# GEGLU feed-forward on one core: the last stage's reload of stored sums as one load, its joins reordered, and the last weight sums loaded ahead of raw weights

## The chip, the cores and the metric

The kernel runs on one core of a Trainium2 chip. The metric is the device time of one execution in microseconds (us). The core has five engines with a queue each: PE (TensorE, matrix products), DVE (VectorE), ACT (ScalarE), POOL (GpSimd) and SP (SyncE, which here only issues DMAs). ACT issues some DMAs too.

## The reference

```python
B, S, Dm, Df = 1, 2048, 1024, 3584        # all bfloat16
g = einsum("bsd,df->bsf", x, w_gate)
u = einsum("bsd,df->bsf", x, w_up)
h = gelu(g) * u                           # tanh form
return einsum("bsf,fd->bsd", h, w_down)
```

Three matrix products: two of 2048 x 1024 by 1024 x 3584, and one of 2048 x 3584 by 3584 x 1024.

## The kernel before

**Products by seven instead of eight.** The kernel works in two passes (`ip` 0 and 1) over 1024 tokens each, in two halves `c` of 512. In each pass the matrices are cut in two along each dimension, and the quadrants of a product come from seven products of sums and differences of blocks in place of eight products of blocks (Winograd's form). For the down product of a pass, `down` (L894), the blocks of `h` are `h(kh, j, c)`: `kh` is the half of Df, `j` one of 14 blocks of 128 rows, `c` the half of tokens. Sums of `h` and of `w_down` are made by DVE while PE multiplies; sums of `w_down` that both passes use are stored in DRAM by pass 0 (`td`) and loaded again in pass 1.

**The stage at issue** is `down` of pass 1, the last 100 us or so. It takes steps; `step()` carries out what `agenda` lists for a step, in the order in which it was entered with `at(last, step, what, ...)`. Steps 0 to 27 are the products of raw blocks, 28 to 30 the first products of sums, 31 to 50 the function `apart` (one of the seven products, done by seven smaller ones again). Steps 51 to 65 go on with the products of sums: at loop index `t` (3 to 17) PE multiplies pair `t` into the banks `e`, and pair `t - 4` into the banks `c`. Steps 66 to 79 are the third loop, `t` = 0 to 13: PE multiplies what `make73` made for `j = t` into `e`, and for 3 <= t < 9 also that of `j = t - 3` into `c`. After the loop come the products of j = 6 to 13 into the four banks of `c`, one bank after the other.

What is prepared for these, and at which step:

- `load12` (L627) loads a pair of stored weight sums `q<-td` on SP (L642); for the last three, j = 11, 12 and 13, at steps 49, 50 and 51 (`LAST12`). `make12` (L645) makes the two sums of `h` that are multiplied by them, on DVE.
- `fetch73` (L658) loads the raw block j of `w_down` on SP (L662), at the step `RAW73[j]`. `make73` (L666) makes from it and from `h` three operands with three DVE instructions and copies the raw block to 32 bit on ACT (`xT<-raw`, L677, or `tb<-raw`, L133), at the step `LAST73[j]`.
- Two quadrants that `apart` and its counterpart in pass 0 gave are stored as halves of words in DRAM tensors `pt`. `turn_back(quad, n)` (L740) loads and transposes them back, eight DMAs (L745) for each of two quadrants: those of quadrant 0, from `pt[0]` and `pt[1]`, are issued from ACT's queue, those of quadrant 1, from `pt[2]` and `pt[3]`, from SP's. `join(quad, i, gt)` (L749) puts halves together on ACT (L750).
- `put_0(i)` (L759) finishes four tiles of the output of pass 0: it joins quadrant 0, adds the sum that pass 0 stored in `ud` and that `fetch_u3` (L755) loads back, on DVE (`st<-gt,u`), and stores the tile. `join_1(i)` (L764) joins quadrant 1 into a tile that the last stores add to `e`.
- `store` (L846) adds two operands on DVE (L121) and issues the tile to the output on SP (L850). The last twelve: four of `e` with `p5`, four of `e` with the joined quadrant 1, and four of `c` with `u2`, each as soon as its bank is done.

**What sets the order.** In this stage the instructions of an engine stand in the order in which the code issues them; each engine takes its queue in order, and an issue on SP that waits holds back all issues behind it. Each DMA is given one of eight completion semaphores in turn, SP's and ACT's together, and is issued only when the DMA that had it before has landed. Tiles come from pools: `kpool` (36 slots) and `spool` (13) for tiles of 128x512, `wpool` (3) for 1 MB tiles. Which slot a tile gets is decided while the program is built, and the first to write a slot waits for the last reader of what was there. In `wpool` go, in this order, the `tid` tiles of `apart`, two 1 MB loads of stored sums (`w<-td`, L631), the transposed words of quadrant 0, those of quadrant 1, and the joined quadrant 1.

Of the kernel before, what the change touches and what calls it, by code (L numbers as in the profile page):

```python
# [10 lines left out]
def kernel(  # L11
# [23 lines left out]
    nc = tc.nc  # L35
    ENG = mybir.EngineType
    ORDER = {ENG.SP, ENG.DVE, ENG.Pool, ENG.PE}
    P = nc.NUM_PARTITIONS
    bf16 = mybir.dt.bfloat16
    f32 = mybir.dt.float32  # L40
# [4 lines left out]
    ADD, SUB, MUL = ALU.add, ALU.subtract, ALU.mult  # L45
# [10 lines left out]
    N = 512  # L56
    NS = N // P
# [17 lines left out]
    LAST12 = [14, 15, 16, 29, 30, None, None, 41, 41, None, None, 49, 50, 51]  # L75
    LAST12S = [16, 18, 20, 34, 37, 40, 43, 45, 47, 49, 51, 53, 55, 57]
    BIG12L = (5, 9)
    RAW73 = [40, 40, 40, 40, 48, 48, 49, 50, 52, 53, 55, 57, 60, 60]
    LAST73 = [52, 53, 55, 57, 59, 61, 63, 65, 66, 68, 70, 71, 72, 73]
    LATE3 = 6  # L80

# [4 lines left out]
    wpool = ctx.enter_context(tc.tile_pool(name="w", bufs=3))  # L86
# [23 lines left out]
    def slot(shape, dtype, name, sums=False):  # L110
        return (spool if sums else kpool).tile(shape, dtype, name=name, tag="s" if sums else "k")
# [8 lines left out]
    def dve(out, a, b, op):  # L120
        nc.vector.tensor_tensor(out=out, in0=a, in1=b, op=op)  # L121
# [29 lines left out]
    def load_w(u, queue=nc.sync):  # L151
        f0 = u * 2 * P
        w = wpool.tile([P, 2, NKB, 2 * P], bf16, name="w")
        for i, src in enumerate((w_gate, w_up)):
            queue.dma_start(
                out=w[:, i],
                in_=src[:, f0 : f0 + 2 * P].rearrange("(ko ki) f -> ki ko f", ki=P),
            )
        return w
# [417 lines left out]
    ud = dpool.tile([P, NS, N], f32, name="ud")  # L577
# [160 lines left out]
    turned = {}  # L738

    def turn_back(quad, n):  # L740
        if n == 0:
            turned["tp", quad] = wpool.tile([P, NS, 2, N], u16, name="w")
        half, i = n // NS, n % NS
        queue = nc.sync if quad else nc.scalar
        queue.dma_start_transpose(  # L745
            out=turned["tp", quad][:, i, half], in_=pt[2 * quad + half][:, i * P : (i + 1) * P]
        )

    def join(quad, i, gt):  # L749
        nc.scalar.copy(  # L750
            out=gt.bitcast(u16).rearrange("p (h d l) -> p h d l", h=2, l=2),
            in_=turned["tp", quad][:, i].rearrange("p h (l d) -> p h d l", l=2),
        )

    def fetch_u3(i):  # L755
        turned["u3", i] = slot([P, N], f32, "u3")
        nc.sync.dma_start(out=turned["u3", i], in_=ud[:, i])

    def put_0(i):  # L759
        gt = slot([P, N], f32, "gt")  # L760
        join(0, i, gt)
        store(0, 1, i, 0, lambda st: dve(st, gt, turned.pop(("u3", i)), ADD))

    def join_1(i):  # L764
        if i == 0:
# [40 lines left out]
    def at(last, step, what, *args):  # L806
        agenda.setdefault((last, int(step)), []).append((what, args))

    for last in (False, True):
# [6 lines left out]
        for j in range(NJ):  # L816
            if (LAST12 if last else AT12)[j] is not None:
                at(last, (LAST12 if last else AT12)[j], load12, j, last)
            at(last, (LAST12S if last else AT12S)[j], make12, j, last)
            at(last, RAW73[j] if last else AT73[j] - 3, fetch73, j)  # L820
            at(last, (LAST73 if last else AT73)[j], make73, j, last)
# [8 lines left out]
        at(1, 2 * i, make_si, i)  # L830
    for n in range(2 * NS):
        at(1, 52 + n // 2, turn_back, 0, n)
        at(1, 59 + n, turn_back, 1, n)
    for i in range(NS):
        at(1, 61 + i, fetch_u3, i)
        at(1, 75 + i, put_0, i)
        at(1, 71 + i, join_1, i)
    moves = [(c, ko) for ko in range(KH) for c in range(2)]
    moves += [(c, ko) for c in (1, 0) for ko in range(KH, NKB)]
    sa = {}  # L840
# [5 lines left out]
    def store(ip, c, i, dc, put):  # L846
        st = slot([P, N], bf16, "st")
        put(st)
        r0 = (2 * ip + c) * N + i * P
        nc.sync.dma_start(out=out2[r0 : r0 + P, dc * N : (dc + 1) * N], in_=st)  # L850
# [177 lines left out]
    w = load_w(1)  # L1028
# [295 lines left out]
```

## Time and profile before

| | |
|---|---|
| median of 3 runs | 538.98 us (538.81 to 541.65) |
| profiled execution, whole | 540.3 us |
| its span, first to last instruction | 538.5 us |
| PE busy | 528.5 us (98%) |
| DVE busy | 404.4 us (75%) |
| ACT busy | 302.0 us (56%) |
| mean granted clock of PE | 0.997 |

The profile is of one execution. An instruction's line number is that of the kernel before, or of a helper (L145 is every product, L121 every addition on DVE). A tile is named without its number: `q` are sums and loaded sums, `w` a 1 MB tile, `st` an output tile, `gt` a joined tile, `bank` a PSUM bank. "x16" is a run of instructions of the same kind merged in one row. Idle time in brackets is that of the engine before the instruction, with what ended it; a wait for several things is put down to the last.

### The profile page before, as it was taken

What the parts mean: (1) busy time and instruction counts of PE and PEld (TensorE: products, weight loads), DVE (VectorE), ACT (ScalarE), POOL (GpSimd) and SP (SyncE); (2) the same over time, 40 slices, a digit from 0 to 9 for tenths busy, and PEclk for the clock granted to TensorE, in tenths of its full rate; (3) what the DMA queues carried; (4) which work ended last, traced back from release to release, by engine and by line L of the source; (5) the groups of instructions that cost most, each with busy time, mean ns of one, the idle gap of its engine ahead of it and who ended that gap; (6) DMA issues with size and microseconds to landing.
All of it is one profiled execution on the core that took longest, in us unless ns stands there. A gap on an engine that the chain in (4) does not pass through costs nothing.

```text
span 538.5 us, 7762 instructions
## 1 busy us (share of the span) xinstructions
PE 528.5 (98%) x2375; PEld 374.9 (70%) x2375; DVE 404.4 (75%) x645; ACT 302.0 (56%) x544; POOL 268.4 (50%) x259
## 2 busy tenths in 40 slices
PE   9999999999999999999999999999999999999994
PEld 5568686868686764688877586766867764777783
DVE  2988768787777786749699887657677599788947
ACT  3557686968686841015576776665666621281652
POOL 1079977979797960000005989695897600000000
PEclk9999999999999999999999999999999999999998
DMA  9695218685777699999997899937354699599764
GB/s 246 150 256 170 79 64 288 197 293 196 234 235 245 224 380 368 356 317 244 248 294 215 288 314 356 253 109 206 97 168 118 225 356 328 163 319 297 189 127 156
DMA packets 141161, 126.09 MB, mean 234 GB/s; under 512 B 31680, under 2 KB 119232, under 8 KB 141120
## 3 DMA queue, kind: packets, MB, share of 16 engines
q1 hardware_dynamic: 136768, 124.55, 76.3%
q10 hardware_dynamic: 4352, 1.05, 1.0%
q8 instruction: 19, 0.31, 0.2%
q14 instruction: 22, 0.18, 0.1%
HBM read 86.38 MB, written 31.06 MB: 218 GB/s over the span
## 4 chain that ended last, share of the span: by engine, by line
PE 89%; DMA 4%; DVE 3%; ACT 2%; issue 1%; SPq 0%; ACTq 0%; DVEq 0%
PE bank L145 88%; DMA w<-pt 2%; DVE q L121 2%; DVE st L121 1%; DMA raw<-in_w_down_dram 1%; ACT gt L750 1%; DMA q<-td 1%; PE bank L1057 1%; PE bank L1002 1%; ACT s L875 0%; ACT xT L733 0%; SPq L662 0%; DVE xT L121 0%; ACTq L1319 0%; ACT u L138 0%
## 5 line engine op out<-in xcount | busy, mean ns | idle before, releaser
L124 POOL TENSOR_TENSOR s<-w 128x512 fp32r<-128x512 bf16 x102 | 117.8, 1176 | 47.5 <-DMA w<-in_w_gate_dram 32.4
L145 PE MATMUL bank<-t,s 128*128 128x512 f32 x528 | 126.3, 392 | 0.0
L145 PEld LDWEIGHTS bank<-t,s 128*128 128x128 f32 x528 | 99.1, 188 | 21.6 <-POOL s L124 0.3
L145 PE MATMUL bank<-xT,w 128*128 128x512 bf16 (+1 forms) x504 | 110.2, 376 | 0.0
L145 PEld LDWEIGHTS <-w 128*128 128x128 bf16 x504 | 47.9, 98 | 58.0 <-issue 4.2
L213 ACT ACTIVATE g<-sum 128x512 f32<-128x512 f32 x81 | 51.5, 636 | 61.0 <-DVE sum L121 60.2
L138 ACT COPY p<-bank 128x512 f32<-128x512 f32 x98 | 55.0, 589 | 46.5 <-PE bank L145 46.4
L121 DVE TENSOR_TENSOR hT<-g,bank 128x512 bf16<-128x512 f32 x72 | 49.0, 687 | 17.6 <-ACT g L213 11.9
L124 POOL TENSOR_TENSOR s<-w,s 128x512 fp32r<-128x512 bf16 x50 | 58.1, 1181 | 0.4
L145 PE MATMUL bank<-q 128*128 128x512 f32 x224 | 56.5, 392 | 1.5 <-DMA q<-td 1.4
L124 POOL TENSOR_TENSOR s<-s,w 128x512 fp32r<-128x512 f32 x50 | 57.5, 1172 | 0.2
L121 DVE TENSOR_TENSOR bank<-bank,p 128x512 f32<-128x512 f32 x74 | 51.3, 695 | 5.7 <-PE bank L145 5.1
L145 PE MATMUL bank<-t,sa 128*128 128x512 f32 x216 | 54.9, 397 | 0.0
L145 PE MATMUL bank<-tb,s 128*128 128x512 f32 x216 | 54.3, 393 | 0.0
L199 POOL COPY seen<-t 128x1 f32<-128x1 f32 x2 | 0.4, 184 | 107.5 <-DVE t L121 107.5
L145 PEld LDWEIGHTS bank<-q 128*128 128x128 f32 x224 | 41.9, 188 | 11.4 <-DVE q L121 1.8
L145 PEld LDWEIGHTS bank<-t,sa 128*128 128x128 f32 x216 | 40.6, 188 | 9.1
L145 PEld LDWEIGHTS bank<-tb,s 128*128 128x128 f32 x216 | 40.5, 188 | 9.0 <-POOL s L124 0.3
L121 DVE TENSOR_TENSOR sum<-bank,p 128x512 f32<-128x512 f32 x54 | 37.0, 686 | 12.0 <-PE bank L145 10.8
L138 ACT COPY u<-bank 128x512 f32<-128x512 f32 x62 | 35.4, 596 | 17.5 <-PE bank L145 13.7
L133 ACT CAST tb<-raw 128x512 fp32r<-128x512 bf16 x20 | 12.3, 624 | 37.3 <-DMA raw<-in_w_down_dram 29.0
L133 ACT CAST sa<-w 128x512 fp32r<-128x512 bf16 x54 | 30.7, 617 | 2.6 <-DMA out_dram<-st 2.6
(121 smaller groups left out, 734.3 us busy)
## 6 DMA issues: line engine op xcount, KB each, us to landing
raw<-in_w_down_dram SPq DMA_DIRECT2D x72, 256.0 KB, 5.9
w<-in_w_gate_dram SPq DMA_DIRECT2D x27, 512.0 KB, 4.8
w<-in_w_up_dram SPq DMA_DIRECT2D x27, 512.0 KB, 6.1
td<-m SPq DMA_DIRECT2D x11, 768.0 KB, 5.0
q<-td SPq DMA_DIRECT2D x28, 256.0 KB, 5.3
pd<-xT SPq DMA_DIRECT2D x10, 512.0 KB, 5.6
w<-td SPq DMA_DIRECT2D x5, 1024.0 KB, 8.6
p<-pd SPq DMA_DIRECT2D x20, 256.0 KB, 4.9
```

What stands on the lines that cost most here:

```text
L121: nc.vector.tensor_tensor(out=out, in0=a, in1=b, op=op)
L124: nc.gpsimd.tensor_tensor(out=out, in0=a, in1=b, op=op)
L133: nc.scalar.copy(out=t, in_=src)
L138: nc.scalar.copy(out=t, in_=ps)
L145: nc.tensor.matmul(ps, lhsT=lhs, rhs=rhs, start=start, stop=stop, skip_group_check=True)
L199: nc.gpsimd.tensor_copy(out=seen, in_=tile[:, :1].bitcast(f32))
L213: nc.scalar.activation(g, src, ACT.Gelu_apprx_tanh)
L750: nc.scalar.copy(out=gt.bitcast(u16).rearrange("p (h d l) -> p h d l", h=2, l=2), in_=turned["tp", quad][:, i].rearrange("p h (l d) -> p h ...
L1002: nc.tensor.transpose(tp[:, ko, :], xn[i][:, ko * P : (ko + 1) * P], ident)
L1057: nc.tensor.matmul(bank[3][:, :cols], lhsT=warm[:, :P], rhs=warm[:, :cols], start=True, stop=True)
```

## The change

The four loads of `ud` become one of 1 MB into a tile of `wpool`, at step 63. Quadrant 0's transposes alternate between its two halves, and its joins and stores (`put_0`) move from steps 75 to 78 to steps 69 to 72, in front of quadrant 1's joins, which move from steps 71 to 74 to steps 74 to 77. Quadrant 1's transposes move from steps 59 to 66 to steps 63 to 70. The raw blocks j = 4 to 11 are loaded up to three steps later and j = 12, 13 one earlier, so that j = 4 and 5 come at the step of the last `load12` and the others behind it.

```diff
-    RAW73 = [40, 40, 40, 40, 48, 48, 49, 50, 52, 53, 55, 57, 60, 60]
+    RAW73 = [40, 40, 40, 40, 51, 51, 52, 53, 54, 55, 56, 57, 59, 59]
...
     def turn_back(quad, n):
         if n == 0:
             turned["tp", quad] = wpool.tile([P, NS, 2, N], u16, name="w")
-        half, i = n // NS, n % NS
+        i, half = n // 2, n % 2
...
-    def fetch_u3(i):
-        turned["u3", i] = slot([P, N], f32, "u3")
-        nc.sync.dma_start(out=turned["u3", i], in_=ud[:, i])
+    def fetch_u3():
+        turned["u3"] = wpool.tile([P, NS, N], f32, name="w")
+        nc.sync.dma_start(out=turned["u3"], in_=ud)
 
     def put_0(i):
         gt = slot([P, N], f32, "gt")
         join(0, i, gt)
-        store(0, 1, i, 0, lambda st: dve(st, gt, turned.pop(("u3", i)), ADD))
+        store(0, 1, i, 0, lambda st: dve(st, gt, turned["u3"][:, i], ADD))
...
     for n in range(2 * NS):
         at(1, 52 + n // 2, turn_back, 0, n)
-        at(1, 59 + n, turn_back, 1, n)
+        at(1, 63 + n, turn_back, 1, n)
     for i in range(NS):
-        at(1, 61 + i, fetch_u3, i)
-        at(1, 75 + i, put_0, i)
-        at(1, 71 + i, join_1, i)
+        at(1, 69 + i, put_0, i)
+        at(1, 74 + i, join_1, i)
+    at(1, 63, fetch_u3)
```

## The prediction

> **What bounds the kernel now.** I read the page first, then the chain of waits from its end backwards, then the timeline of the last 60 us, and last what the built programs of both kernels say each instruction waits for.
>
> ```profile
> span 538.5 us, 7762 instructions
> ...
> PE 528.5 (98%) x2375; PEld 374.9 (70%) x2375; DVE 404.4 (75%) x645; ACT 302.0 (56%) x544; POOL 268.4 (50%) x259
> ```
>
> PE is the bound: 538.5 - 528.5 leaves 10 us in which it does nothing. The chain of waits (start, length, what) says where those lie:
>
> ```profile
> 488.98 6.61 DMA w<-pt
> ...
> 495.66 3.58 DMA q<-td
> 499.23 0.14 issue
> 499.37 9.33 PE bank L145 x40
> ...
> 523.58 4.31 ACT gt L750 x4
> ...
> 531.60 4.18 DVE st L121 x7
> ```
>
> Two places. At 499.37 PE resumes after a load of stored weight sums (q<-td), whose issue had waited for a transposing DMA (w<-pt). From 523.58 on the chain leaves PE: joins on ACT, then stores on DVE. The timeline shows both, with the idle time before an instruction in brackets:
>
> ```profile
> 489.64 0.68 DVE L121 TENSOR_TENSOR q<-raw 128x512 fp32r<-128x512 bf16 x1
> 490.53 3.79 PE L145 MATMUL bank<-w,q 128*128 128x512 f32 x16
> 491.56 0.69 DVE L121 TENSOR_TENSOR q<-q,hT 128x512 fp32r<-128x512 f32 x1
> 494.70 0.69 DVE L121 TENSOR_TENSOR q<-q,hT 128x512 fp32r<-128x512 f32 x1
> 495.97 1.07 PE L145 MATMUL bank<-q 128*128 128x512 f32 x4
> 499.37 1.16 PE L145 MATMUL bank<-q 128*128 128x512 f32 x4 [1.43 <-DMA q<-td]
> 524.69 0.69 DVE L121 TENSOR_TENSOR st<-gt,u 128x512 bf16<-128x512 f32 x1 [8.05 <-ACT gt L750]
> 529.26 1.53 PE L145 MATMUL bank<-tb,q 128*128 128x512 f32 x6
> 535.10 0.68 DVE L121 TENSOR_TENSOR st<-bank,u 128x512 bf16<-128x512 f32 x1
> ```
>
> PE's last product ends at 529.26 + 1.53 = 530.79. The last store on DVE starts only at 535.10, because sixteen stores of 0.60 us each stand in a row from 524.69, and four of them (st<-gt,u, those of put_0) waited 8.05 us for ACT. What follows the last store start is fixed: 538.5 - 535.1 = 3.4 us.
>
> **1. The tail: put_0 ahead of the last sums.** In the changed program the four put_0 stand one by one between the triples that make73 makes for j = 9 to 13, so they leave the queue in front of the last twelve stores. They still cost 4 x 0.60 = 2.4 us of DVE. Their cover is the time in which DVE waits now (8.05 us); without it they would delay the sums that PE multiplies last. With twelve stores left, the first starts when the e sums are done (523.45 now) and eight of them take 4.9 us, to about 528.4; the four c stores then follow PE's quarters, and the last starts 0.05 us after PE's end. So the tail gives back 535.10 - 530.84 = 4.26 us as long as PE ends when it does now. What is late next is PE itself.
>
> **2. One load in place of four.** SP now issues four u<-ud (0.52, 0.53, 1.58 and 0.52 us) between transposes; they go, and one issue of 1 MB comes. It stands behind all raw loads and one transpose of pt2, and its issue waits for an earlier DMA on its completion semaphore (there are eight, handed out in turn) and for the product t = 10. I work out raw loads at 0.5 us an issue from 497.5, the transpose at 502.7 and this load at 503.9. Landing: the 1 MB loads w<-td took 6.9 and 8.6 us, the 256 KB loads u<-ud 3.6 to 4.7; 503.9 plus 5 to 8.6 is 509 to 512.5, and I take 510 because most raw loads have landed by then. The first put_0 is due on DVE at 510.9 (step 4). DVE is in order: behind it stand the sums for j = 10 to 13. The last of them is then made by 520.0, and PE wants it at 522.39 + 0.93 = 523.3, so the load may land 3.3 us late, at 514.2, for nothing.
>
> **3. The second quadrant.** Its transposes (1.12 us each on SP) run from about 502.7 to 513.2 instead of 504.4 to 519.6; its joins come last on ACT, four of 1.1 us, behind the cast that now waits for PE's c product of step t = 6 (516.1), so 516.7 to 521.2. DVE wants the first at about 526.3. Hidden, with 5 us in hand.
>
> **4. The loads of stored sums, and a reused buffer.** Here I look for what PE waits for at 499.37. The first two pairs of td loads (j = 11, 12) do move ahead of the raw loads, but the pair for j = 13, the one that PE waited for, still stands behind two raw loads and the pt2 writes. Its first issue now waits for the sixth of the eight transposes on ACT's queue. These transposes start earlier: the first shared a semaphore with a raw load that landed at 488.83 and now follows a load long landed, so it starts after ACT's cast at 484.64 + 0.62 = 485.3, not at 488.98. At 1.28 us each plus a cast in between the sixth starts at 492.5. If it lands in 2.9 to 5.3 us (SP's lone transposes took 2.7, ACT's later ones 4.3 to 5.3), the pair is issued at 495.4 to 497.8, 0.5 us apart, and the half that PE needs first lands 3.1 to 3.6 us after its own issue: 499.0 to 501.9. I take 499.2, since the raw traffic that slowed the present ones has moved behind. That alone is no gain on 499.23.
>
> The second part is a wait that the diff does not show. The pool gives the weight difference that make73 makes for j = 2 (the DVE instruction at 489.64) another buffer: that of the sum for j = 6, which PE reads until the end of the sixteen products of 490.53, at 494.32. Before, its buffer was long free. So this instruction starts at 494.36, 4.7 us later, and all that is queued behind it on DVE shifts. Two of those PE waits for. The sum for j = 12 starts 491.56 - 489.64 = 1.92 us after it and takes 0.69: 496.97, plus 0.2 for the weight load, 497.2 against PE's 495.97: 1.2 us of stall. The next eight products (1.82 us) end at 499.0. The sum for j = 13 starts 494.70 - 489.64 = 5.06 us after it: 500.11, plus 0.2, 500.3: 1.3 us more. PE thus resumes at 500.3 instead of 499.37: 0.93 us later than now, the present stall of 1.43 us being replaced by two of 2.5 us together. The cost is bounded by -1.43 (neither wait binds) and by the late end of the load, 501.9 + 0.1 - 499.37 = 2.6.
>
> After that DVE has no idle time until 520.7 (eighteen instructions of 0.604 us from 500.02 bring it to 510.9), and every raw load is due 2 us or more before its use. PE ends at 530.79 + 0.93 = 531.7.
>
> **5. Sum.** -4.26 (tail) + 0.93 (PE) = -3.3 us: a span of 535.2. The profiled execution took 540.3, its span and 1.8 us around it; 537.0 after. It was 1.3 us above the median of 538.98; the same saving from the median gives 535.6, or -0.6%. A change of 0.5%, 2.7 us, is about what a measurement of this kernel can tell from none: that line lies at 536.3, or a PE delay of 1.55 us in place of 0.93.
>
> **Rivals.**
>
> *Late weight sums* (PE delay of 1.55 to 7 us, no change to tell). If ACT's sixth transpose takes the 6.61 us of the first one now, it lands at 499.1; the pair's second half goes out at 499.6 and lands at 503.2 (3.6) to 504.8 (5.25, its twin's time): delay 3.9 to 5.5, time 538.6 to 540.2. For it: one DMA's landing frees the next issue all through this stretch. Against: 6.61 was with seven loads queued ahead, and those are gone. Such a wait is one gap of PE of about 4 to 5 us, and the clock could go with it. The row: PE stops at 530.79, and the granted clock holds until inside the second of these slices (the last three columns are clock, DMA share, GB/s):
>
> ```profile
> 534.00:535.00 1.00, 0.00 (x0) 0.00 (x0) 1.00 (x2) 0.00 (x0) 0.00 (x0) 1.00 0.57 194
> 535.00:536.00 1.00, 0.00 (x0) 0.00 (x0) 0.78 (x2) 0.00 (x0) 0.00 (x0) 0.82 0.65 217
> ```
>
> 0.82 is 0.36 us at half, so it fell at 535.64, 4.85 us after the last product; a gap below that costs nothing more by this row. [...]
>
> *No new wait binds* (delay under 0.5 us). The pool's buffer is free in time or PE is not as tightly fed as I read: PE resumes with the load at 499.3, time 534.6; with the load early too, PE ends at 529.4 and the time is 533.2. Against it stands a wait that is in the built program.
>
> *The single load blocks DVE* (slower). Four loads gave each put_0 its own landing; now all four hang on one, in front of sums that PE needs. Past 514.2 each us late is a us of the end. Slower by 0.5% (541.7) needs a landing after 520.3. With the pair landing at 504.8, the raw halves behind it, the load issued at 509 and 8.6 us of flight, it lands at 517.6 and the time is 539.0; it takes one more link of 3 us in SP's chain.
>
> *The change does not do what it says.* Partly so for the sums of j = 13, and that is in the forecast.
>
> **Numbers.** Forecast (delay 0.5 to 1.55, 534.9 to 536.3): 0.52. No new wait: 0.14. Late sums: 0.26. Blocked DVE, slower: 0.08. Faster by over 0.5% is the first two, 0.66; the same 0.26; slower 0.08. The range goes from the middle of the early case, 533.9, to the lower half of the late one, 538.4; it leaves out about 0.05 below and 0.15 above.
>
> **What would show it.** In the profile after: four st<-gt,w on DVE between 510 and 520 and no wait for ACT ahead of 524; the last DVE store within 0.1 us of PE's last product; an idle DVE of some 4 us ahead of the q<-raw after 489.6, released by PE; two gaps of PE between 496 and 500.5, released by DVE and not by q<-td; the 1 MB load landing before 512. One PE gap released by q<-td after 501 makes the late rival right; a DVE wait for the w<-ud load makes the blocked one right; no DVE wait at 490 to 494 makes step 4 wrong.

## The result, and the profile after

The changed kernel is slower: 543.12 us median (542.01 to 544.36, 10 runs) against 540.81 (538.37 to 541.66, 10 runs) for the kernel before, measured beside it. The ratio is 1.0053, 95% interval 1.0033 to 1.0072. The forecast was 535.6 us, range 533.9 to 538.4. It was counted from a median of 538.98 (3 runs), so what compares is its -0.6% with the +0.5% measured. The profiled execution took 542.01 us.

First the page of the changed kernel: its span, and what its engines were busy for.

```profile
span 540.2 us, 7756 instructions
...
PE 530.9 (98%) x2375; PEld 376.4 (70%) x2375; DVE 404.5 (75%) x645; ACT 302.1 (56%) x544; POOL 268.3 (50%) x259
```

PE executes the same 2375 products as before and is busy 2.4 us longer: some of them ran at a lower clock. The chain of waits (start, length, what) says where the end was decided:

```profile
493.24 2.90 DMA w<-pt
...
496.87 6.19 DMA q<-td
503.06 0.14 issue
503.19 33.69 PE bank L145 x136
536.88 0.02 issue
536.91 0.69 DVE st L121
```

After 503.19 there is nothing but PE, and one store behind it: the tail that the change went for is gone. In front of it stands the same link as before, a load of stored sums behind a transpose, and it now releases PE 3.8 us later. The timeline shows the rest:

```profile
490.32 3.79 PE L145 MATMUL bank<-w,q 128*128 128x512 f32 x16
494.15 0.69 DVE L121 TENSOR_TENSOR q<-raw 128x512 fp32r<-128x512 bf16 x1 [4.63 <-PE bank L145]
495.09 1.01 SPq L662 DMA_DIRECT2D raw<-in_w_down_dram  x2
496.20 1.05 SPq L642 DMA_DIRECT2D q<-td  x2
496.82 1.21 PE L145 MATMUL bank<-q 128*128 128x512 f32 x4 [0.90 <-DVE q L121]
499.28 0.69 DVE L121 TENSOR_TENSOR q<-q,hT 128x512 fp32r<-128x512 f32 x1
503.19 2.05 PE L145 MATMUL bank<-q 128*128 128x512 f32 x4 [4.23 <-DMA q<-td]
514.68 0.69 DVE L121 TENSOR_TENSOR st<-gt,w 128x512 bf16<-128x512 f32 x1 [1.34 <-ACT gt L750]
535.34 1.52 PE L145 MATMUL bank<-tb,q 128*128 128x512 f32 x6
536.91 0.69 DVE L121 TENSOR_TENSOR st<-bank,u 128x512 bf16<-128x512 f32 x1 [1.14 <-PE bank L145]
```

The DVE wait of 4.63 us for PE is the reused buffer of step 4, and it costs PE a first stall of 0.90 us. The second stall, due near 499 for a sum on DVE, is hidden under a larger one: PE stands for 4.23 us until the load lands. The four products at 503.19 then take 2.05 us where such a row took 1.16 before. The stretches (PE, PEld, DVE, ACT, POOL busy; then granted clock, DMA share, GB/s) say why:

```profile
502.00:504.00 2.00, 0.81 (x2) 0.74 (x3) 1.58 (x3) 0.00 (x1) 0.00 (x0) 0.50 1.05 324
504.00:506.00 2.00, 2.00 (x6) 1.52 (x6) 0.72 (x2) 2.00 (x5) 0.00 (x0) 0.50 1.02 327
506.00:508.00 2.00, 2.00 (x6) 1.55 (x5) 1.78 (x3) 1.08 (x3) 0.00 (x0) 0.51 1.06 350
508.00:510.00 2.00, 2.00 (x10) 1.65 (x9) 1.56 (x3) 0.00 (x0) 0.00 (x0) 1.00 0.77 170
```

The granted clock is one half until 508, and PE does 6 products in 2 us in place of 10.

**The sum.** Traces start some tenths apart, so I count from a common event, the start of the sixteen products `bank<-w,q`, to the last DVE store. Before: 535.10 - 490.53 = 44.57 us. Forecast: 3.33 less, 41.24. After: 536.91 - 490.32 = 46.59. PE was to resume 500.3 - 490.53 = 9.77 us into this stretch and resumed at 503.19 - 490.32 = 12.87, which is 3.10 late; from there the last store was to start 41.24 - 9.77 = 31.47 us later and started 33.72 later, which is 2.25 of lost clock. 3.10 + 2.25 = 5.35, the whole difference between 41.24 and 46.59.

### The profile page after: what moved, and what is told of

It reads as the page before. It is cut to its first block, busy times and chain, and to the rows that moved or that the text cites. A ratio compares the mean times of both kernels' runs of the same rounds, so it can differ in the third digit from the quotient of the medians.

```text
span 540.2 us, 7756 instructions
## 1 busy us (share of the span) xinstructions
PE 530.9 (98%) x2375; PEld 376.4 (70%) x2375; DVE 404.5 (75%) x645; ACT 302.1 (56%) x544; POOL 268.3 (50%) x259
## 4 chain that ended last, share of the span: by engine, by line
PE 93%; DMA 2%; DVE 2%; ACTq 1%; ACT 1%; issue 0%; SPq 0%; DVEq 0%
PE bank L145 92%; ACTq L745 1%; DMA q<-td 1%; DVE q L121 1%; PE bank L1057 1%; DMA w<-pt 1%; DVE xT L121 1%; PE bank L1002 1%; ACT s L875 0%; ACT xT L733 0%; ACT u L138 0%; DVE st L121 0%; ACT xT L677 0%; SPq L642 0%; ACTq L733 0%
```

## The experiments

Each ran in a group with the kernel before, and its ratio is against that. "Stretch" is the time just defined.

**`e1_tail_only`: the change without the new order of raw loads.**

```diff
-    RAW73 = [40, 40, 40, 40, 51, 51, 52, 53, 54, 55, 56, 57, 59, 59]
+    RAW73 = [40, 40, 40, 40, 48, 48, 49, 50, 52, 53, 55, 57, 60, 60]
```

> The change without its new load order (RAW73 as before); joins, transposes and the single 1 MB load as changed. Theory A (the loss is the load order: the last pair of sums lands late and PE's clock falls; the tail is a real gain): PE stalls at about 499.4 as in the kernel before, ends at 530.8, the last store follows at once, span about 534.3, 4 us (0.8%) under the kernel before. Theory B (the single load and the put_0 in front of the sums block DVE and so PE): DVE waits for the load ahead of the first put_0, PE loses products behind t = 9, span at or above 538.5.

535.54 us, ratio 0.9928 [0.9915, 0.9941], span 534.6, stretch 39.76: 4.81 us less than before. Of these, 3.70 lie between PE's resuming at 499.22 and the last store, where step 1 had 4.26; the other 1.11 are PE resuming that much earlier in the stretch. The tail's edits alone are a real gain.

```profile
499.22 1.16 PE L145 MATMUL bank<-q 128*128 128x512 f32 x4 [0.31 <-DMA q<-td]
513.47 0.69 DVE L121 TENSOR_TENSOR st<-gt,w 128x512 bf16<-128x512 f32 x1 [4.22 <-DMA w<-ud]
522.65 1.20 PE L145 MATMUL bank<-q 128*128 128x512 f32 x4 [0.22 <-DVE q L121]
```

The pair of sums is hardly waited for. DVE waits 4.22 us for the 1 MB load, and the idle time of PE behind that is 0.22 us.

**`e2_raw_only`: the new order of raw loads in the kernel before,** that is the first line of the change's diff and no other.

> The kernel before with the new load order alone (RAW73). Theory A: the last pair lands at about 503 as in the changed kernel, the clock falls to half for some 6 us, PE ends near 536.9; the stores then wait for PE and not for the joins, so the span is about that of the changed kernel, 540.2 (0.3 to 0.5% over the kernel before), although nothing of the tail is moved. Theory B: as the kernel before, 538.5, since what it blames is not in this kernel.

542.17 us, ratio 1.0056 [1.0034, 1.0078], stretch 45.62.

```profile
495.15 0.69 DVE L121 TENSOR_TENSOR q<-raw 128x512 fp32r<-128x512 bf16 x1 [4.63 <-PE bank L145]
497.83 1.21 PE L145 MATMUL bank<-q 128*128 128x512 f32 x4 [0.90 <-DVE q L121]
503.86 1.15 PE L145 MATMUL bank<-q 128*128 128x512 f32 x4 [3.89 <-DMA q<-td]
```

The wait for the buffer, the stall and the late pair are all there without any edit of the tail, and `e1_tail_only` has no DVE wait for PE near 494. So they come with the new order of raw loads: this one line of load steps turns the -0.7% of the tail alone into +0.5%.

**`e3_warm32` and `e7_warm44`: PE kept busy in the gap.** The changed kernel with products by zeros ahead of the step of j = 13, 32 and then 44 of them:

```diff
+            if last and t == NJ - 1:
+                for _ in range(32):
+                    matmul(e[0][:, : 2 * P], zero[:, :P], zero, False, False)
```

> The changed kernel with 32 products of zeros by zeros (128x256, bf16) added into bank e[0] just ahead of the products that wait for the last pair; they add nothing to the sums and fill some 3.5 of the 4.2 us of the gap. Theory A with the clock (half clock after the gap costs 2.3 us by itself): granted clock stays at 1.00 after 501, PE ends at about 534.6, span about 538.0, 2.2 us under the changed kernel. Without the clock (the late pair alone explains the loss, or the clock falls for another reason): clock still falls near 501.6, span 540.2 or a little more.

541.13 us, ratio 1.0041 [1.0023, 1.0059]. The profile didn't settle it. In that execution, the slowest of the eleven, the pair landed later still, PE idled 3.10 us behind the zeros, and the clock fell all the same, to 0.50 from 507.13 to 510.54. But 8 of its 11 runs have a mean clock of 0.999 or 1.000 and took 540.0 to 542.2 us, and the other three have 0.996 and took 543.6 to 544.2.

> The changed kernel with 44 products by a tile of zeros ahead of the step of j = 13, added to a sum that they do not alter (44 x 0.115 = 5.1 us of PE), so that PE is busy in the gap before the late pair whether it lands at 503 or at 505. Theory A (the clock fell because PE stood idle for over 2.6 us): PE starts the zeros near 499.2, ends them near 504.3, goes on within 1.5 us, the granted clock stays 1.00 from 500 to 530, and from the first product of j = 13 to PE's last end it takes 31.4 to 31.6 us instead of 33.7; span 538.8 to 539.5, ratio 1.000 to 1.003. Theory B (the clock falls for another reason here, such as the DMA traffic or the fp32 products): it falls to one half after 501 with the zeros in place, 33.7 us from resume to end, and the ratio is 1.005 to 1.009, as the zeros then delay PE by 1 us more.

541.23 us, ratio 1.0024 [1.0009, 1.0038]; the mean clock is 1.000 in all 10 runs.

```profile
500.00:502.00 2.00, 2.00 (x19) 1.76 (x19) 1.90 (x4) 0.62 (x1) 0.00 (x0) 1.00 1.24 278
502.00:504.00 2.00, 2.00 (x21) 1.79 (x19) 2.00 (x4) 0.62 (x1) 0.00 (x0) 1.00 0.89 271
504.00:506.00 2.00, 2.00 (x14) 1.54 (x12) 1.46 (x3) 0.47 (x1) 0.00 (x0) 1.00 0.98 286
506.00:508.00 2.00, 2.00 (x10) 1.64 (x9) 1.39 (x3) 2.00 (x6) 0.00 (x0) 1.00 0.97 304
```

PE is busy throughout and the clock stays. The products of j = 13 start at 505.02 and the last store at 536.51, 31.49 us later in place of the changed kernel's 33.72, though the same DMAs run beside it. So the idle gap took the clock, at 2.23 us. The late pair is still there: the span, 539.8, is 0.3 us above what theory A expected. The fill is no cure: it holds PE until 505, and the stretch, 44.92, is still longer than before.

**`e5_pair_first`: all pairs of last sums ahead of the pt2 writes and the raw loads,** in the changed kernel:

```diff
-    LAST12 = [14, 15, 16, 29, 30, None, None, 41, 41, None, None, 49, 50, 51]
+    LAST12 = [14, 15, 16, 29, 30, None, None, 41, 41, None, None, 49, 49, 49]
```

> The changed kernel with one list edited so that all three pairs of last stored sums, j = 11 to 13, go out at step 49, ahead of the pt2 writes and of the raw loads; the reused buffer, and with it the wait of the weight difference for j = 2, stays. Theory A (the loss is the late landing of the pair for j = 13 and the clock that fell in that gap; the buffer wait alone costs what step 4 of the prediction said): the pair now follows an early transpose on ACT's queue, which landed by 491.8 in the changed kernel, and lands before 498; DVE still waits 4 to 5 us for PE near 494; PE stalls near 496 and 499 for DVE alone, 2 to 2.5 us together, no gap is long enough for the clock, and PE's last products end 5 us earlier than in the changed kernel (2.9 for the landing, 2.25 for the clock): span 534.8 to 535.8, ratio 0.994 to 0.996. Theory B (the buffer wait costs more than its two stalls, since all of DVE shifts): PE stalls for DVE again after 505, ratio 0.998 or more. Theory C (moving loads here only moves the lateness to the pt2 writes and the transposes): ACT's casts wait behind the transposes, a sum for j = 13 is late for a cast as in e4_tail_p47, ratio near 1.001.

537.64 us, ratio 0.9959 [0.9942, 0.9975], span 536.0, stretch 41.87, and no loss of clock: the mean is 1.000.

```profile
494.67 0.69 DVE L121 TENSOR_TENSOR q<-hT,q 128x512 fp32r<-128x512 bf16 x1 [4.05 <-PE bank L145]
496.74 1.21 PE L145 MATMUL bank<-q 128*128 128x512 f32 x4 [0.30 <-DVE q L121]
499.94 1.19 PE L145 MATMUL bank<-q 128*128 128x512 f32 x4 [1.07 <-DVE q L121]
514.97 0.69 DVE L121 TENSOR_TENSOR st<-gt,w 128x512 bf16<-128x512 f32 x1 [1.55 <-DMA w<-ud]
524.14 1.19 PE L145 MATMUL bank<-q 128*128 128x512 f32 x4 [0.60 <-DVE q L121]
```

This is the picture that the prediction drew of the changed kernel: both gaps of PE are released by DVE. PE resumes 499.94 - 490.84 = 9.10 us into the stretch, against 8.84 before and 9.77 in the forecast: that is 0.26 us late in place of 0.93. Another DVE instruction stands at the head of the wait here, so that 0.60 us less of it reaches PE in the first stall (0.30 for 0.90). The pair landed at 498.84, later than the expected 498 but ahead of DVE's sum. The load for put_0 landed at 514.85, past the 514.2 up to which the prediction called it free, and there PE lost 0.60 us. The span came 0.2 us above what was expected.

**`e9_pair_before_raws`: only the raw loads of j = 4 and 5 taken from in front of the pair,** which stays behind the pt2 writes:

```diff
-    RAW73 = [40, 40, 40, 40, 51, 51, 52, 53, 54, 55, 56, 57, 59, 59]
+    RAW73 = [40, 40, 40, 40, 52, 52, 52, 53, 54, 55, 56, 57, 59, 59]
```

> The changed kernel with the raw loads of j = 4 and 5 taken from step 51 to step 52, so that the pair of sums for j = 13 stays behind the pt2 writes and beside the transposes, but no raw load stands in front of it; the reused buffer stays. Open is what made the pair's second load fly 6.19 us where the forecast had 3.1 to 3.6. Theory A (the two raw loads issued 1.1 and 0.5 us ahead of it): it now flies 3.3 to 4.2 us, lands by 500.5, PE resumes for DVE's sum near 500 or within 0.6 us of it, the clock holds, the ratio is 0.995 to 0.998, as e5_pair_first. Theory B (the DMA transposes on ACT's queue, two of which fly beside it as before): 5.5 to 6.5 us, it lands at 501.3 to 502.5, PE idles for 2.3 to 3.5 us, the clock falls where that is over 2.6 us, ratio 0.998 to 1.005.

541.35 us, ratio 1.0012 [0.9991, 1.0032]: not to be told from before. The load that PE needs flew 5.38 us (chain of waits):

```profile
496.50 5.38 DMA q<-td
501.88 0.14 issue
502.01 34.21 PE bank L145 x136
```

So the flight is long without the two raw loads too, and theory A falls. Theory B's landing, gap and ratio hold (the flight is just under its 5.5), but the transposes by themselves aren't the reason: in `e5_pair_first` and `e10_pair_first_four` the same load flew 3.40 and 3.36 us beside transposes of its own, issued 0.07 and 0.17 us ahead of it. What it has ahead in `e9_pair_before_raws` and not there is a pt2 write issued 1.4 us earlier and the pair's first half 0.9 us earlier. These don't settle it either, since the flight differs as much between executions with the same order of issues (pt2 write, two raw loads, pair). The chains of `e2_raw_only` and of `e3_warm32` have:

```profile
499.27 4.46 DMA q<-td
498.43 7.45 DMA q<-td
```

With the 6.19 us of the changed kernel that is 4.5 to 7.5 us for one order. In `e7_warm44` the pair was issued as late as 501.0 and flew 3.2 to 3.4. What makes the flight long stays open. What does go with the place in the queue is the landing, counted from the start of the stretch: 12.4 to 15.1 us in the four kernels with two raw loads ahead of the pair, 10.8 in `e9_pair_before_raws`, 8.0 and 10.0 with the pair first, 8.7 before.

**`e4_tail_p47`: `e1_tail_only` with the last three entries of `LAST12` at 47.**

> As the tail alone (RAW73 as before), and all three last pairs of stored sums are loaded at step 47, ahead of the raw blocks and of the transposes on ACT's queue (LAST12 ends 47, 47, 47). Theory A: the last pair lands by 492.5, no wait for it at all, so the present stall of 1.43 us goes too: PE ends at about 529.4, span about 533, 1% under the kernel before. If a raw block or a reused buffer becomes the next wait: 533.5 to 535.5. Theory B: no gain on the kernel before.

540.23 us, ratio 1.0015 [1.0002, 1.0028]: worse than `e1_tail_only`. The pair is no longer waited for, but what it passed is:

```profile
493.43 0.62 ACT L677 CAST xT<-raw 128x512 fp32r<-128x512 bf16 x1 [8.41 <-DMA pt<-xT]
499.36 0.69 DVE L121 TENSOR_TENSOR q<-hT,hL 128x512 fp32r<-128x512 bf16 x1 [3.38 <-ACT xT L677]
500.89 1.20 PE L145 MATMUL bank<-q 128*128 128x512 f32 x4 [3.21 <-DVE q L121]
```

ACT's casts stand in its queue behind transposes that were issued late; DVE waits for a cast, PE for DVE, and the clock is 0.50 from 502.05 to 505.46. The early load wasn't free here: ACT's queue hung on those it overtook.

**`e8_tail_p49`: the same pairs at step 49 instead.**

> e1_tail_only (the tail's edits alone, raw loads as before the change) with all three pairs of last stored sums at step 49, ahead of the pt2 writes. Theory A: in e1_tail_only PE waited 0.31 us for q<-td and 0.71 for a sum on DVE near 499; the first goes, the second stays unless ACT's cast comes earlier: 0.3 us gain or none, ratio 0.991 to 0.993, not to be told from e1_tail_only. Theory C (as in e4_tail_p47, earlier pairs push the pt2 writes, the transposes and ACT's casts later): a sum on DVE waits for an ACT cast by 2 us or more, PE stalls over 2.6 us and its clock falls, ratio 0.998 to 1.002.

534.49 us, ratio 0.9903 [0.9886, 0.9921], a little under the expected 0.991 to 0.993. In the chain of waits PE runs in one piece from 485.02:

```profile
485.02 46.23 PE bank L145 x201
531.28 0.69 DVE st L121
```

The stretch is 38.62 us: no wait of PE is left in it. Two steps divide this from `e4_tail_p47`.

**`e6_four_loads`, `e10_pair_first_four` and `e11_tail_p49_four`: the single load taken apart** in `e1_tail_only`, `e5_pair_first` and `e8_tail_p49`:

```diff
-        nc.sync.dma_start(out=turned["u3"], in_=ud)
+        for i in range(NS):
+            nc.sync.dma_start(out=turned["u3"][:, i], in_=ud[:, i])
```

> e1_tail_only with the 1 MB load of the first quadrant's stored sums taken apart again into four loads of 256 KB, one behind the other at the same step and into the same tile. Theory A (the place of the put_0 brings the gain, not the size of the load; the load has slack): ratio 0.991 to 0.995, as e1_tail_only; the four issues push the second quadrant's transposes back by 1.5 to 3 us, hidden, since the first of its joins has some 5 us; the first put_0 waits less than the 4.2 us that it waited for w<-ud there. Theory B (the single load is part of the gain, by three issues fewer on SP's queue and on its completion semaphores): the last join_1 or the last c stores wait for the transposes, the last store comes 1 to 3 us behind PE's end, ratio 0.995 to 0.999.

535.03 us, ratio 0.9913 [0.9898, 0.9929], stretch 38.61; DVE no longer waits for w<-ud.

> e5_pair_first with the 1 MB load taken apart into four of 256 KB. There the load flew 6.92 us and landed at 514.85, later than the 514.2 up to which the prediction called it free, the first put_0 waited 1.55 us for it, and PE lost 0.60 us to a sum near 524. Theory A (a late single load holds up DVE and through it PE): the first quarter lands by 512.5, no wait for w<-ud stands on DVE or one under 0.5 us, the 0.60 us near 524 go, and PE takes 32.0 to 32.2 us from the first product of j = 13 to its end in place of 32.71: ratio 0.994 to 0.996. Theory B (the 0.60 us come from the buffer wait's shift of DVE by itself): PE still waits 0.4 us or more for DVE near 524, ratio 0.995 to 0.997.

537.90 us, ratio 0.9958 [0.9942, 0.9973]. The first quarter landed at 511.80, no `st<-gt,w` waits for w<-ud, and the 0.60 us near 524 are gone, as theory A has it; the ratio doesn't tell this from `e5_pair_first`. The 32.0 to 32.2 us expected of PE weren't met: 33.07, since in this execution the pair landed at 500.33, PE idled 2.16 us and the clock fell; the clock at half for 3.41 us costs 1.7 of these, which leaves 31.4. That is 1.3 us under the 32.71 of `e5_pair_first`, of which the 0.60 are less than half; the rest isn't explained.

> The two edits that did no harm together: the tail's edits alone, raw loads as before the change, all pairs of last sums at step 49, four loads of 256 KB. Both e6_four_loads and e8_tail_p49 had PE without a gap from 485 to its end (46.23 us in each), so there is nothing left for either to take away there. Theory A: ratio 0.989 to 0.993, not to be told from those two; PE runs 46.2 us in one piece. Theory B (the two interact, transposes of the second quadrant come too late): the last join ends after 524, the last store comes 1 us or more behind PE's end, ratio 0.993 to 0.997.

535.38 us, ratio 0.9913 [0.9896, 0.9931], stretch 38.61. Four loads do as well as one in every pairing. `e1_tail_only`, `e6_four_loads`, `e8_tail_p49` and `e11_tail_p49_four` are 0.7 to 1.0% faster than the kernel before, and their intervals overlap.

## Why the prediction was wrong

**Step 1, the tail: right.** The last store starts 0.03 us after PE's end in the changed kernel. From PE's resuming to the last store it took 535.10 - 499.37 = 35.73 us before and, with the clock held, 31.49 in `e7_warm44`: 4.24 us less, where step 1 had 4.26.

**Step 2, the one load: right in its flight and its risk, wrong in its issue.** Issued at 508.43 (forecast 503.9), it landed at 513.64 after 5.21 us, inside the bounds for its flight but past the forecast 509 to 512.5. The ten raw loads ahead of it were issued from 499.30 and not 497.5, and took 6.93 us and not 5: SP waited 3.8 us for transposes to land. The first put_0 waited for ACT's join instead. That a landing past 514.2 is paid for showed in `e5_pair_first`: 0.65 us past it, and 0.60 us of PE. One price of the blocked rival can't hold by the prediction's own terms: with the pair landing at 504.8 PE alone is 5.5 us late, which the first rival puts at 540.2, so the 539.0 is too low.

**Step 3, the second quadrant: right.** Its joins ended on ACT at 526.23, 5 us later than forecast, and the stores at the end never waited for them.

**Step 4, the wait for the buffer: right,** 4.63 us for 4.7, a first stall of 0.90 us for 1.2. Without the late pair the sum for j = 13, made at 499.28 + 0.69 = 499.97, would have let PE go on near 500.0, for 500.3: PE started 0.05 us behind the sum for j = 12 (496.77 to 496.82), where step 4 added 0.2 for a weight load. Not every raw load was 2 us early, and DVE was not busy throughout until 520.7: casts on ACT waited 1.20 and 0.73 us for raw loads, and DVE 1.69 us for PE and 1.34 for the join. PE shows no wait for any of these.

**Step 4, the pair for j = 13: this is the step that failed.** Its issue was forecast well: the first half at 496.20, inside 495.4 to 497.8. Its flight was not: 6.19 us, where step 4 took "3.1 to 3.6 us after its own issue" and chose the early end, "since the raw traffic that slowed the present ones has moved behind". The reason doesn't hold. Two raw loads still stood in front of it, as the prediction itself says, where the last one ahead of it before had been issued 9 us earlier, and a pt2 write had come closer. The 3.58 us that it took over from the kernel before belonged to a half issued 3.36 us behind its twin (492.30 and 495.66); here the halves went out 0.67 us apart and flew 6.2 us each. That the place in the queue makes the pair land late is shown by `e2_raw_only` and `e5_pair_first`; which of the transfers around it made this flight so long isn't (`e9_pair_before_raws`). The bound of 501.9 was passed by 1.2 us.

**The second term that failed is the clock.** From before's last idle stretch the prediction read that "a gap below that costs nothing more", that being 4.85 us. A gap of 4.23 cost 2.25 us. The row was no bound: in the changed kernel the clock fell 2.19 us after PE stopped (498.96 to 501.15). Neither the sum of step 5 nor the late rival's 538.6 to 540.2 has anything in it for the clock.

**The rival "late weight sums" is what happened,** one gap released by q<-td after 501, with the sign that the clock gives it: 4.03 us later in the stretch than before (12.87 - 8.84), plus 2.25, minus 4.26 for the tail, is +2.02. It held 0.26. Had the flight been taken at the 5.25 us of its twin, with the issue that step 4 chose, PE would have resumed near 501.5 and the sum been -2.2 us, inside the 2.7 that step 5 calls no change to tell.

## What to carry to other kernels

When a load that PE waits for changes its place in a queue, look at what flies with it at its new place, its own twin and the writes too; a flight from the old place isn't its price, and one order of issues gave flights 3 us apart. Price a gap of PE with the clock in it: here one of 4.2 us cost 6.5. A change in two halves that share a queue can hide a gain behind a loss, so run each half alone.

## What the runs showed of the clock

In six of the profiled executions the clock fell to half for 3.41 us or for twice that. The edges follow from quarter-microsecond stretches, where a clock of 0.80 in 0.25 us means a fall 0.6 of the way through (0.6 at full clock and 0.4 at half make 0.80). For the changed kernel:

```profile
501.00:501.25 0.25, 0.00 (x0) 0.00 (x0) 0.25 (x2) 0.02 (x1) 0.00 (x0) 0.80 0.62 206
...
507.75:508.00 0.25, 0.25 (x2) 0.18 (x1) 0.03 (x1) 0.00 (x0) 0.00 (x0) 0.55 1.21 355
```

It fell at 501.15 and came back at 507.98: 6.83 us. For `e10_pair_first_four`:

```profile
501.00:501.25 0.25, 0.25 (x2) 0.24 (x1) 0.00 (x0) 0.00 (x0) 0.00 (x0) 0.61 1.12 365
504.25:504.50 0.25, 0.25 (x2) 0.15 (x2) 0.25 (x2) 0.25 (x2) 0.00 (x0) 0.57 1.12 356
```

501.06 to 504.46: 3.41 us, half as long. Read in the same way, the falls of `e2_raw_only` (505.08 to 508.49), `e3_warm32` (507.13 to 510.54) and `e4_tail_p47` (502.05 to 505.46) lasted 3.41 us too, and that of `e9_pair_before_raws` 6.83 (501.05 to 507.88). The mean clocks leave room for little more at half: with these falls alone they would be 0.997 in `e2_raw_only`, `e3_warm32` and `e4_tail_p47` and 0.994 in `e9_pair_before_raws`, and 0.996 and 0.993 are measured, which is up to 1.5 us more as an estimate from these numbers.

In four of the six the fall came only after PE had resumed: 0.60 us after in `e10_pair_first_four` (resumed at 500.46), 1.22 in `e2_raw_only` (503.86), 1.12 in `e3_warm32` (506.01) and 1.16 in `e4_tail_p47` (500.89). So it doesn't answer to the gap of the moment. In these four PE was busy all through the half clock, and it ended after 3.41 us. In the two others PE idled for the first part of it, 0.96 us in `e9_pair_before_raws` and 2.04 in the changed kernel, and it lasted 6.83. Half of the changed kernel's other 4.79 us is 2.4, for the 2.25 counted above.

Counting 3.41 us back from each fall, PE idled 1.96 us of them in `e9_pair_before_raws`, 2.16 in `e10_pair_first_four`, 2.19 in the changed kernel and in `e2_raw_only`, and up to 2.30 in the other two. In the 3.41 us ahead of those it idled 1.70 in `e2_raw_only`, and at their end, 501.66, the clock was 1.00. The length of a gap doesn't decide by itself: in `e10_pair_first_four` one of 2.16 us was enough, in the changed kernel's tail PE stood for 3.3 us to the end of the span (536.88 to 540.2) at a clock of 1.00, and in before's tail the clock held for 4.85. What decides isn't shown by these traces. The 2.6 us that some expectations name as a limit fit a fall of the changed kernel's clock at 501.6, where the expectation of `e3_warm32` puts it, 0.45 us too late; no run shows such a limit.

The runs of one kernel differed in their clock. Only the profiled execution of a kernel shows its gap; the others show their mean clock. Half a clock for 3.41 us in 540 lowers the mean by 0.003, for 6.83 by 0.006. Of the 12 runs of `e9_pair_before_raws` two have a mean clock of 1.000 (537.0 and 539.1 us), seven 0.996 or 0.997, three 0.993 or 0.994 (541.4 to 543.4). The changed kernel, with a gap of 4.2 us in its profile, has 0.993 or 0.994 in nine of ten runs and never 1.000.
